# Key norms read from the diagonal of K K^T, queues reordered at the start, and expert weights split without extra copies

## The chip, the cores and the metric

One Trainium2 chip, one core of it. The metric is the device time of one execution in microseconds. In the text PE is the tensor engine (PEld its weight loads), DVE the vector engine, ACT the scalar engine, POOL the GpSimd engine and SP the engine that issues the DMAs.

## What is computed

A delta-rule attention over 4 batches x 8 heads, 768 positions, head size 48, and on its output a dense layer pair 384 -> 2048 -> 384 with softplus between. Cut to what matters:

```python
k_n = k / (norm(k) + 1e-6)
for t in range(768):
    y[t] = q[t] @ state
    v_old = state applied to k_n[t]
    state += beta[t] * outer(k_n[t], v[t] - v_old)
x = y as (3072, 384)
h = x @ w_in
g = maximum(h, 0) + log1p(exp(-abs(h)))
out = g @ w_out
```

`w_in` and `w_out` come as float64 words (`wts`, seen as pairs of int32) and are turned into float32 on the chip.

## The kernel before, in words

**Attention.** The 768 positions are cut into 12 chunks `s` of 64. Inside a chunk the recurrence is a triangular system per head; two chunks make a pair `u`, and the systems of a pair, 32x32 blocks of all heads, are inverted together on DVE. Steps of a chunk: `gram` (products K K^T: the diagonal 32x32 blocks go to `LTD`, the block below them to `OFF`), `norms` (squares on ACT, a row sum on DVE, then a root by Ln and Exp on ACT and one Newton step on DVE; from it the scale `cT` = beta / norm^2 and its negative `ncT`), `invert` (a transpose of `LTD` into `lq`, a mask from POOL times `ncT`, then a substitution loop, L224 and L230), `finish` (two transposes into `tt`), for the first two pairs `join` (the substitution ran over 16x16 blocks there), then `cross_a`, `arrange`, `cross_b`, `keys`, `mask_keys`, `u_all`, `y_all` and `state`. `y_all` leaves the chunk's output as `x` and, for a quarter of the heads, as `x4`, which six small DMAs (L377) lay into `x`.

**The dense layers** (`moe`) take the same 12 chunks of rows, each in 8 groups of two weight slices `f`: products into `ph` (L479), softplus (L483 to L485 on ACT, L493 or L487 on DVE), products into `po` (L462). Chunk 0 multiplies in plain float32 by `HF`; chunks 1 to 11 use three products of split operands (`W` with high and low part).

**Weights.** `weights` converts slice after slice, four DVE passes (L410, L413, L417, L420) between an ACT pass (L398) and an ACT copy into `HF` (L423). `split`, called in chunk 1, copies `HF` on ACT (L430), casts the copy to the high part on ACT (L432) and subtracts on DVE (L433). A one-column DVE copy (L408) holds the load of slice f + AHEAD back until the conversion has come so far.

**What sets the order.** Everything up to the first chunk's output is written out by hand in one block, `with tc.manual_schedule(...)`: there the engines named keep the order of the code, and `fill(n)` puts n steps of the weight conversion in between. Behind it, `attend` and `invert_some` deal attention units and substitution steps out over the groups of the dense layers (`RATE`, `LEAD`, `FIRST`), and a scheduler lays the instructions of an engine in order. Each engine runs its own list in order.

Of the kernel before, what the change touches and what calls it, by code (L numbers as in the profile page):

```python
# [30 lines left out]
AHEAD = 4  # L31
# [4 lines left out]
def deltanet_moe(ctx, tc, kT, qT, kN, kI, vN, beta, wts, out):  # L36
# [35 lines left out]
    bet = const.tile([P, NS, NP], F32, name="bet")  # L72
# [37 lines left out]
    def copy_diagonals(s, pas):  # L110
        u, j = divmod(s, 2)
        for e in range(2):
            nc.scalar.copy(parity(LTD[u][:, j * NP:(j + 1) * NP])[:, e], pas[e][:, :, 0:HB])

    def copy_below(s, pas):
        for e in range(2):
            for h in range(2):
                nc.scalar.copy(parity(OFF[s])[hi[h], e], pas[e][hi[h], :, 0:HB])

    def gram(s):  # L120
        if s not in OFF:
            OFF[s] = two.tile([P, NP, HB], F32, name="off", bufs=3)
# [7 lines left out]
        u, j = divmod(s, 2)  # L130
        for e in range(2):
            nc.scalar.copy(parity(LTD[u][:, j * NP:(j + 1) * NP])[:, e], pas[e][:, :, 0:HB])
        for e in range(2):
            nc.scalar.copy(parity(OFF[s])[:, e], pas[e][:, :, HB:])

    def gram_diagonal(s, pool, name):
        pas = [pool.tile([P, NP // 2, HB], F32, name=name) for e in range(2)]
        for half in (lo, hi):
            for i, e, p, ab, t in quads:
                k = kts[s % 3][dr[ab], p, half[0].start:half[0].stop]  # L140
                nc.tensor.matmul(pas[e][half[t], i, :], k, k, start=True, stop=True)
        copy_diagonals(s, pas)

    def gram_below(s):
        OFF[s] = two.tile([P, NP, HB], F32, name="off", bufs=3)
        pas = [ps_a.tile([P, NP // 2, HB], F32, name="pa") for e in range(2)]
        for i, e, p, ab, t in quads:
            k = kts[s % 3][dr[ab], p, :]
            nc.tensor.matmul(pas[e][hi[t], i, :], k[:, HB:C], k[:, 0:HB], start=True, stop=True)
        copy_below(s, pas)  # L150

    def norms(u, kas=None):

        ss = one.tile([P, 2 * NP], F32, name="ss")
        for j in range(2):
            ka = kas[j] if kas else load_ka(2 * u + j)
            if not kas:
                yield
            nc.scalar.activation(ka, ka, AF.Square)
            yield  # L160
            nc.vector.tensor_reduce(ss[:, j * NP:(j + 1) * NP], ka, op=ALU.add, axis=AX.X)
            yield
        x0 = one.tile([P, 2 * NP], F32, name="rt")
        r0 = one.tile([P, 2 * NP], F32, name="r0")
        nn = two.tile([P, 2 * NP], F32, name="nn")
# [19 lines left out]
        return cT, ncT

    def invert(u, cT, ncT):
# [5 lines left out]
        lq = one.tile([P, HB, HB], F32, name="ltq")  # L193
        for a in blocks:
            nc.gpsimd.affine_select(
                out=Z[:, a:a + n, a:a + n],
                in_=ncT[:, a:a + n].unsqueeze(1).to_broadcast([P, n, n]),
                compare_op=ALU.is_gt, fill=0.0, base=0, pattern=[[1, n], [-1, n]],
                channel_multiplier=0)
        nc.vector.transpose(lq.rearrange("p j i -> p i j"), LTD[u].rearrange("p q i -> p i q"))  # L200
        yield
        for a in blocks:
            d = (slice(None), slice(a, a + n), slice(a, a + n))
            nc.vector.tensor_tensor(lq[d], lq[d], Z[d], op=ALU.mult)
# [86 lines left out]
    def keys(s, e):  # L291

        kt = kts[s % 3]
        for g in range(2):
            pk = ps_a.tile([P, 4, QW], F32, name="pa")
            for i, f, p, ab, t in quads:
                if f == e and i // 4 == g:
                    nc.tensor.matmul(pk[tk[t], i % 4, :], kt[dr[ab], p, :], bv[dr[ab], ab, p, :],  # L298
                                     start=True, stop=True)
            r = parity(NV[s])[:, e, 4 * g:4 * g + 4]  # L300
            nc.vector.tensor_tensor(r, r, pk[:, :, C:], op=ALU.subtract)  # L301
            PK[s, e, g] = pk

    def mask_keys(s, e):

        for g in range(2):
            pk = PK.pop((s, e, g))
            for ab in range(2):
                t = tk[ab ^ e]
                nc.vector.tensor_tensor(  # L310
                    be[tk[ab], ab, e, 4 * g:4 * g + 4, 0:C], pk[t, :, 0:C],
# [37 lines left out]
    def y_all(s):  # L349
# [21 lines left out]
        if s + 1 < NS:  # L371
            load_q(s + 1)
        if n == 2:
            x, x4 = x.bitcast(F32), x4.bitcast(F32)
        for hh in range(NK):
            for ab in range(2):
                nc.sync.dma_start(x[ab * C + D:(ab + 1) * C, :, hh],  # L377
                                  x4[ab * C + 16 * hh:ab * C + 16 * hh + 16])
        return last


    def load_weights(f):
        if f not in ST:
            ST[f] = one.tile([P, 4 * DM], I32, name=f"w{f}")
        nc.sync.dma_start(ST[f], wts[f])

    def weights():
# [8 lines left out]
        def magnitude(f):  # L396
            ex = two.tile([P, 2 * DM], I32, name="ex", bufs=3)
# [3 lines left out]
        ex = magnitude(0)  # L401
        yield
        for f in range(NF):
            hw, lw = words(f)
            if f + AHEAD < NF:

                ST[f + AHEAD] = one.tile([P, 4 * DM], I32, name=f"w{f + AHEAD}")
# [7 lines left out]
            after = magnitude(f + 1) if f + 1 < NF else None  # L415
# [8 lines left out]
            done[0], ex = f + 1, after  # L424
            yield

    def split(f):

        hf = two.tile([P, 2 * DM], F32, name="ex", bufs=3)
        nc.scalar.copy(hf, HF[f])  # L430
        w = W[f] = one.tile([P, 2, 2 * DM], F32R, name=f"w{f}")
        nc.scalar.copy(w[:, 0], hf)  # L432
        nc.vector.tensor_tensor(w[:, 1], hf, w[:, 0], op=ALU.subtract)  # L433


    def moe():
# [4 lines left out]
        for s in range(NS):  # L441
# [10 lines left out]
            def outp(f0, g, po=po, s=s, weight=weight):  # L452
# [64 lines left out]
    cols = {}  # L517
# [11 lines left out]
    def chunk(s):  # L529
        more = s % 2 == 0 and 2 <= s < NS - 2  # L530
        if s % 2 == 0:
            load_v(s + 1)
            if more:
                load_k(s + 2)
                nm = norms(s // 2 + 1)
                next(nm)
            yield from begin(s)
        for e in range(2):
            keys(s, e)
        for e in range(2):  # L540
            mask_keys(s, e)
# [6 lines left out]
        if more:  # L548

            for _ in range(3):  # L550
                next(nm)
        yield
        last = y_all(s)
        if s + 1 < NS:
# [3 lines left out]
        if s + 1 < NS:  # L558
            state(s)
            load_ki(s + 1)  # L560
            if more:
                with tc.issue_after(last[0].ins):
                    next(nm)
                with tc.issue_after(last[1].ins):
                    next(nm)
            yield
        if more:
# [4 lines left out]
            cols[u] = run(nm)  # L572
# [3 lines left out]
            background.append(invert(u, *cols[u]))  # L576

    background, softplus = [], [None]
# [8 lines left out]
    kas = [one.tile([P, 2, NP, D], F32, name=name) for name in ("tt", "x2")]  # L587
    kas = [[t[:, j] for j in range(2)] for t in kas]
    with tc.manual_schedule(engines={ET.PE, ET.DVE, ET.Activation, ET.Pool}):
        for s in range(2):  # L590
            load_k(s)
            nc.sync.dma_start(kas[0][s], kN[s])
# [24 lines left out]
        nm = norms(0, kas[0])  # L617
        for _ in range(5):
            next(nm)
        gram_diagonal(0, ps_a, "pa")  # L620
        gram_diagonal(1, ps_a, "pa")
        cols[0] = run(nm)
        iv = invert(0, *cols[0])
        next(iv)
# [10 lines left out]
        for _ in range(5):  # L635
# [160 lines left out]
```

## Time and profile before

| | us |
|---|---|
| median of 3 runs | 676.06 |
| lowest, highest of 3 runs | 675.17, 678.13 |
| the profiled execution | 672.85 |
| its span in the trace | 671.10 |
| PE busy, share of the span | 611.4, 91% |
| DVE busy | 462.2, 69% |
| ACT busy | 362.1, 54% |

A row of a list of groups names the source line, the engine, the operation, what it writes from what it reads, then the busy time, the mean duration of one instruction, and the idle time of the engine ahead of it with what ended it. "Issue" there is time in which an engine waited for nothing that the profile shows. A float32 product shows in the records twice. The granted clock is a share of the full TensorE clock.

### The profile page before, as it was taken

How to read it: one execution, taken by the hardware profiler on the slowest of the kernel's cores; microseconds unless marked ns; L12 is line 12 of the kernel's file. 1: busy time of each engine (PE TensorE's matmuls, PEld its weight loads, DVE VectorE, ACT ScalarE, POOL GpSimd, SP SyncE). 2: the span in 40 equal slices, each digit the busy share in tenths (PEclk: the TensorE clock that was granted, in tenths of full speed). 3: DMA queues.
4: the chain of work that ended last, by engine and by line, in shares of the span. 5: the costliest groups of instructions: out<-in, count | busy, mean ns of one | idle time of the engine just before them, and what ended most of it. 6: DMA issues, size and time to landing. Idle time of an engine off the chain costs nothing.

```text
span 671.1 us, 22732 instructions
## 1 busy us (share of the span) xinstructions
PE 611.4 (91%) x10032; PEld 570.8 (85%) x10032; DVE 462.2 (69%) x1036; ACT 362.1 (54%) x667; POOL 30.4 (5%) x56
## 2 busy tenths in 40 slices
PE   4356987988989999989999999999999998999997
PEld 3345765678879999979999999998999997999997
DVE  4946499997556986558987559984559884544443
ACT  4234658889563447453555654555545546364433
POOL 3100010000000001000001000001000001000000
PEclk9999887998998999999999999996999998999999
DMA  9826267000131020141211321201202100200000
GB/s 230 272 94 164 101 214 208 0 26 3 51 93 63 26 60 27 49 109 48 58 40 39 92 66 48 60 25 50 61 14 66 30 25 4 61 24 13 3 23 24
DMA packets 35091, 44.73 MB, mean 67 GB/s; under 512 B 21776, under 2 KB 27184, under 8 KB 34992
## 3 DMA queue, kind: packets, MB, share of 16 engines
q1 hardware_dynamic: 34992, 43.27, 22.6%
q8 instruction: 79, 1.29, 0.8%
q14 instruction: 20, 0.16, 0.1%
HBM read 36.27 MB, written 4.72 MB: 61 GB/s over the span
## 4 chain that ended last, share of the span: by engine, by line
PE 77%; DVE 8%; issue 6%; ACT 6%; DMA 2%; SPq 1%; DVEq 0%; ACTq 0%
PE ph L479 28%; PE po L462 28%; PE pa L298 4%; PE pa L359 4%; PE pa L344 2%; PE pa L128 2%; PE pa L285 2%; PE pa L332 2%; PE pa L264 1%; DVE big L310 1%; PE pa L254 1%; ACT tt L276 1%; DMA ka<-kN 1%; DVE tt L237 1%; DMA kt<-kT 1%
## 5 line engine op out<-in xcount | busy, mean ns | idle before, releaser
L479 PE MATMUL ph<-x,w 128*128 128x256 f32 x1680 | 240.5, 294 | 6.1 <-ACT w L423 4.3
L479 PEld LDWEIGHTS ph<-x,w 128*128 128x128 f32 x1680 | 224.0, 192 | 14.7 <-ACT w L423 5.0
L462 PE MATMUL po<-w,gh 128*128 128x384 f32 x768 | 207.0, 355 | 2.1 <-DVE gh L493 1.6
L483 ACT ACTIVATE a<-ph 128x512 f32<-128x512 f32 x96 | 57.4, 598 | 167.7 <-PE ph L479 164.4
L462 PEld LDWEIGHTS po<-w,gh 128*128 128x128 f32 x768 | 134.9, 190 | 12.0 <-DVE gh L493 2.4
L487 DVE SCALAR_TENSOR_TENSOR a<-ph,a 128x512 f32<-128x512 f32 x88 | 60.5, 689 | 107.0 <-ACT a L485 105.9
L462 PE MATMUL po<-w,gl 128*128 128x384 f32 x352 | 119.5, 340 | 0.0
L462 PEld LDWEIGHTS po<-w,gl 128*128 128x128 f32 x352 | 66.5, 189 | 0.6 <-DVE gl L490 0.2
L490 DVE TENSOR_TENSOR gl<-a,gh 128x512 fp32r<-128x512 f32 x88 | 60.8, 691 | 3.3 <-DVE Z L230 0.2
L484 ACT ACTIVATE a<-a 128x512 f32<-128x512 f32 x96 | 60.8, 633 | 2.7
L485 ACT ACTIVATE a<-a 128x512 f32<-128x512 f32 x96 | 60.7, 632 | 2.3
L230 DVE TENSOR_TENSOR Z<-Z,work 128x84 f32<-128x84 f32 (+14 forms) x148 | 44.2, 306 | 2.9
L224 DVE TENSOR_TENSOR work<-Z,ltq 128x84 f32<-128x84 f32 (+14 forms) x148 | 44.1, 305 | 2.4
L489 DVE CAST gh<-a 128x512 fp32r<-128x512 f32 x88 | 37.5, 427 | 7.8 <-PE po L462 5.6
L298 PE MATMUL pa<-big,kt 48*64 48x112 f32 x704 | 39.3, 284 | 0.0
L310 DVE TENSOR_TENSOR big<-pa,maskP 64x256 f32<-64x256 f32 x88 | 37.0, 420 | 1.4
L298 PEld LDWEIGHTS pa<-big,kt 48*64 48x64 f32 x704 | 35.2, 148 | 1.7 <-issue 0.8
L336 ACT COPY big<-pa 64x384 f32<-64x384 f32 x46 | 21.6, 472 | 26.7 <-PE pa L332 26.0
L359 PEld LDWEIGHTS pa<-big 128*64 128x64 f32 x768 | 28.9, 154 | 5.4 <-ACT big L336 2.0
L359 PE MATMUL pa<-big 128*64 128x64 f32 x768 | 32.0, 243 | 1.5 <-ACT big L336 1.2
L278 POOL MEMSET tt<- 32x512 f32 x24 | 13.1, 544 | 400.3 <-PE pa L264 219.3
L301 DVE TENSOR_TENSOR nv<-nv,pa 128x192 f32<-128x192 f32 x44 | 15.3, 352 | 19.1 <-PE pa L298 18.3
(101 smaller groups left out, 611.9 us busy)
## 6 DMA issues: line engine op xcount, KB each, us to landing
w<-wts SPq DMA_DIRECT2D x16, 768.0 KB, 5.9
kt<-kT SPq DMA_DIRECT2D x24, 192.0 KB, 3.6
big<-qT SPq DMA_DIRECT2D x24, 192.0 KB, 3.8
nv<-vN SPq DMA_DIRECT2D x12, 384.0 KB, 3.4
ki<-kI SPq DMA_DIRECT2D x24, 192.0 KB, 3.5
out<-ex SPq DMA_DIRECT2D x24, 192.0 KB, 1.9
ka<-kN SPq DMA_DIRECT2D x8, 384.0 KB, 3.9
x<-x SPq DMA_DIRECT2D x66, 32.0 KB, 2.4
```

What stands on the lines that cost most here:

```text
L224: nc.vector.tensor_tensor(tmp[:, a:a + r, 0:j], Z[:, a + j + 1:a + n, a + j:a + j + 1].to_broadcast([P, r, j]), lq[:, a + j:a + j + 1, a:a ...
L230: nc.vector.tensor_tensor(z, z, tmp[:, a:a + r, 0:j], op=ALU.add)
L298: nc.tensor.matmul(pk[tk[t], i % 4, :], kt[dr[ab], p, :], bv[dr[ab], ab, p, :], start=True, stop=True)
L310: nc.vector.tensor_tensor(be[tk[ab], ab, e, 4 * g:4 * g + 4, 0:C], pk[t, :, 0:C], maskP[t].unsqueeze(1).to_broadcast([C, 4, C]), op=ALU.mult)
L359: nc.tensor.matmul(py[tk[ab], i, :], big[:, at + C:at + 2 * C], big[:, at:at + C], start=True, stop=True)
L462: nc.tensor.matmul(po[:, h, 0:DM], g[b][:, f - f0, h * P:(h + 1) * P], weight(f, a, DM, DM), start=(f == 0 and i == 0), stop=end)
L479: nc.tensor.matmul(ph[:, f - f0], weight(f, a, k * P, P), xr[b][k], start=(c == 0), stop=(c == len(terms1) * NK - 1))
L483: nc.scalar.activation(a, ph, AF.Abs)
L484: nc.scalar.activation(a, a, AF.Exp, scale=-1.0)
L485: nc.scalar.activation(a, a, AF.Ln, bias=1.0)
L487: nc.vector.scalar_tensor_tensor(a, ph, 0.0, a, op0=ALU.max, op1=ALU.add)
L490: softplus[0] = nc.vector.tensor_tensor(g[1], a, g[0], op=ALU.subtract)
```

## The change

- **Norms.** The array `kN`, its loads, the squares and the row sums are gone. `gram_heads` multiplies each head's whole 48x64 key block with itself: 32 products of 64x64 in a chunk, where `gram` had 64 products with 32 weight columns. `invert` transposes `LTD` first, then a strided copy takes the diagonal as the squared norms, POOL clears the diagonal and what lies above it in place, and `norms` goes on in the transposed layout. All of it is now part of the inversion's own steps.
- **Copies of the gram.** A 64x64 product holds its two diagonal blocks in different columns, so `copy_diagonals` makes three copies where one was; for the first two chunks ACT and DVE take half of them each.
- **Start.** SP is now in the hand-written block. The keys of chunks 0 and 1 are loaded first, then weight slice 0; `load_q(1)` stands behind the six small `x` DMAs of chunk 0; the first group of the dense layers stands ahead of `join(1)`; conversion steps are dealt out anew.
- **Weights.** The last conversion pass writes in place into `ST[f]`, which then is `HF[f]`; `split` casts and subtracts straight from it. Slice f lives in buffer `w{f+1}`, so `W[0]` has a free buffer at once, and each later `W[f]` takes the buffer of the slice ahead of it. AHEAD is 3, it was 4.

The core of the diff:

```diff
-    def gram(s):
-        for i, e, p, ab, t in quads:
-            k = kts[s % 3][dr[ab], p, :]
-            for half, order in ((lo, k), (hi, k.rearrange("d (b c) -> d b c", b=2)[:, ::-1, :])):
-                first = half[0].start
-                nc.tensor.matmul(pas[e][half[t], i, :], k[:, first:first + HB], order,
-                                 start=True, stop=True)
+    def gram_heads(s):
+        pas = [ps_a.tile([P, NP // 2, C], F32, name="pa") for e in range(2)]
+        for i, e, p, ab, t in quads:
+            k = kts[s % 3][dr[ab], p, :]
+            nc.tensor.matmul(pas[e][tk[t], i, :], k, k, start=True, stop=True)
+        return pas
...
+            copies[e](ltd[:, e], pas[e][:, :, HB:])
+            for h in range(2):
+                copies[e](ltd[lo[h], e], pas[e][lo[h], :, 0:HB])
...
-            nc.scalar.activation(ka, ka, AF.Square)
-            nc.vector.tensor_reduce(ss[:, j * NP:(j + 1) * NP], ka, op=ALU.add, axis=AX.X)
+        nc.vector.tensor_copy(ss, lq.rearrange("p j i -> p (j i)")[:, 0:HB * HB:HB + 1])
...
-    def invert(u, cT, ncT):
-            nc.gpsimd.affine_select(out=Z[:, a:a + n, a:a + n], in_=ncT[:, a:a + n]...
+    def invert(u):
+        nc.vector.transpose(lq.rearrange("p j i -> p i j"), LTD[u].rearrange("p q i -> p i q"))
+        yield
+        nm = norms(u, lq)
+        next(nm)
+            nc.gpsimd.affine_select(out=lq[d], in_=lq[d], compare_op=ALU.is_gt, fill=0.0, ...
+        cT, ncT = yield from nm
...
-        if s + 1 < NS:
+        if 0 < s < NS - 1:
             load_q(s + 1)
         ...
+        if s == 0:
+            load_q(1)
...
-            nc.vector.scalar_tensor_tensor(ex, lw, 29, ex, op0=ALU.logical_shift_right,
+            nc.vector.scalar_tensor_tensor(ST[f][:, 0:2 * DM], lw, 29, ex, op0=ALU.logical_shift_right,
                                            op1=ALU.bitwise_or)
-            HF[f] = one.tile([P, 2 * DM], F32, name=f"w{f}")
-            nc.scalar.copy(HF[f], ex.bitcast(F32))
+            HF[f] = ST[f][:, 0:2 * DM].bitcast(F32)
...
-        hf = two.tile([P, 2 * DM], F32, name="ex", bufs=3)
-        nc.scalar.copy(hf, HF[f])
         w = W[f] = one.tile([P, 2, 2 * DM], F32R, name=f"w{f}")
-        nc.scalar.copy(w[:, 0], hf)
-        nc.vector.tensor_tensor(w[:, 1], hf, w[:, 0], op=ALU.subtract)
+        nc.scalar.copy(w[:, 0], HF[f])
+        nc.vector.tensor_tensor(w[:, 1], HF[f], w[:, 0], op=ALU.subtract)
...
         y_all(0)
+        load_k(3)
+        load_v(1)
+        fill(5)
+        state(0)
+        load_ki(1)
+        next(mg)
         jn = join(1)
```

How the lists of the engines move, at the three places that the prediction speaks of.

**DVE, the start of its list.** Before, up to the transpose of the first pair's blocks (`ss` holds the squared norms, `nn` the norms, `ltq` the transposed blocks):

```order
L161 TENSOR_REDUCE ss<-tt 128x16 x2
L166 TENSOR_SCALAR rt<-ss 128x32
L170 RECIPROCAL r_132<-rt 128x32
L171 TENSOR_TENSOR r_132<-r_132,ss 128x32
L172 TENSOR_TENSOR r_132<-r_132,rt 128x32
L173 TENSOR_SCALAR nn<-r_132 128x32
L177 TENSOR_TENSOR r_132<-nn 128x32
L178 RECIPROCAL r_132<-r_132 128x32
L179 TENSOR_TENSOR r_132<-r_132,bet 128x32
L183 STREAM_TRANSPOSE cT<-r_132 128x32
L184 TENSOR_SCALAR ncT<-cT 128x32
L200 STREAM_TRANSPOSE ltq<-work 128x32x32
```

The same place in the changed kernel:

```order
L116 COPY work<-pa 128x8x32
L118 COPY work<-pa 32x8x32 x2
L116 COPY work<-pa 128x8x32
L118 COPY work<-pa 32x8x32 x2
L166 STREAM_TRANSPOSE ltq<-work 128x32x32
L133 COPY ss<-ltq 128x32
L138 TENSOR_SCALAR rt<-ss 128x32
L388 COPY w_217<-ex 128x1
L390 TENSOR_SCALAR ex<-ex 128x768
L393 TENSOR_SCALAR ex<-ex 128x768
L142 RECIPROCAL r_206<-rt 128x32
L143 TENSOR_TENSOR r_206<-r_206,ss 128x32
```

The transpose stood behind the norms and now stands ahead of them; copies of the gram come first, and one slice's first two conversion passes stand where DVE waits for ACT's Ln and Exp.

**PE, from chunk 0's output to the first products of the dense layers.** Before (L359 is `y_all`, L247 and L254 are `join`, L344 is `state`, L479 the dense layers):

```order
L359 MATMUL pa<-big 64x64 x32
L247 MATMUL pa<-tt,x_303 32x16 x64
L344 MATMUL pa<-big,ki 48x48 x32
L254 MATMUL pa<-x_303,tt 32x16 x64
L479 MATMUL ph<-x_847,w_706 128x256 x3
```

The same place in the changed kernel (L336 is `y_all`, L321 `state`, L457 the dense layers, L225 and L232 `join`):

```order
L336 MATMUL pa<-big 64x64 x32
L321 MATMUL pa<-big,ki 48x48 x32
L457 MATMUL ph<-x_664,w_89 128x256
L457 MATMUL ph<-x_664,w_104 128x256
L457 MATMUL ph<-x_664,w_89 128x256
L457 MATMUL ph<-x_664,w_104 128x256
L457 MATMUL ph<-x_664,w_89 128x256
L457 MATMUL ph<-x_664,w_100 128x256 x3
L225 MATMUL pa<-tt,x_284 32x16 x64
```

`join(1)`, 128 products, stood between chunk 0's output and the first dense products and now stands behind the first group of them.

**DVE, inside the conversion.** In the changed kernel, some ten conversion passes after the first softplus (L390, L393, L398 and L401 are the four passes, L411 the subtraction of `split`, whose line before was L433):

```order
L393 TENSOR_SCALAR ex<-ex 128x768
L398 SCALAR_TENSOR_TENSOR ex<-w_617,ex 128x768
L411 TENSOR_TENSOR w_1498<-w_100,w_1498 128x768
L401 SCALAR_TENSOR_TENSOR w_617<-w_617,ex 128x768
L388 COPY w_969<-ex 128x1
L411 TENSOR_TENSOR w_1501<-w_104,w_1501 128x768
L390 TENSOR_SCALAR ex<-ex 128x768
L94 TENSOR_TENSOR nv<-nv,nn 128x768
```

Before, one L433 stood ahead of the last conversion pass of all 16 slices, and 15 behind it; now 13 subtractions stand ahead of it and 3 behind it.

## Rows read from the trace of the kernel before

**Rows 1.** Windows: stretch, then each engine's busy us, granted clock, DMA share, GB/s.

```profile
0.00:67.00 67.00, 32.42 (x1409) 29.03 (x1409) 43.06 (x114) 24.73 (x48) 10.71 (x26) 0.98 0.67 190
67.00:129.00 62.00, 54.16 (x653) 41.35 (x647) 52.86 (x101) 43.94 (x74) 3.93 (x6) 0.89 0.46 142
...
134.00:206.00 72.00, 64.37 (x1583) 59.96 (x1581) 49.49 (x121) 49.43 (x89) 3.51 (x5) 0.94 0.16 44
206.00:671.00 465.00, 455.67 (x6380) 437.16 (x6380) 311.84 (x683) 239.07 (x449) 12.25 (x19) 0.98 0.16 43
```

**Rows 2.** Timeline, PE, up to the first dense products: start, us, line, count, idle before.

```profile
4.93 1.84 PE L141 MATMUL pa<-kt 48*32 48x32 f32 x126 [0.84 <-DMA kt<-kT]
...
20.85 2.08 PE L318 MATMUL ph<-big,kt 48*64 48x64 f32 x34 [4.16 <-issue]
...
28.93 0.61 PE L247 MATMUL pa<-tt,x 32*32 32x16 f32 x28
...
33.70 1.57 PE L247 MATMUL pa<-tt,x 32*32 32x16 f32 x100 [4.16 <-issue]
...
35.73 0.61 PE L254 MATMUL pa<-x,tt 32*32 32x16 f32 x28 [0.46 <-ACT x L249]
39.22 1.57 PE L254 MATMUL pa<-x,tt 32*32 32x16 f32 x100 [2.88 <-issue]
...
66.34 0.73 PE L254 MATMUL pa<-x,tt 32*32 32x16 f32 x39 [3.19 <-issue]
67.00 6.39 PE L479 MATMUL ph<-x,w 128*128 128x256 f32 x20
```

**Rows 3.** Timeline, DVE, the first pair's norms and inversion.

```profile
11.88 0.35 DVE L170 RECIPROCAL r<-rt 128x32 f32<-128x32 f32 x1 [0.56 <-ACT rt L168]
...
14.34 2.12 DVE L200 STREAM_TRANSPOSE ltq<-work 128x1024 f32<-128x1024 f32 x1
...
19.57 0.24 DVE L224 TENSOR_TENSOR x<-Z,ltq 128x14 f32<-128x14 f32 x2
...
26.32 1.95 DVE L236 STREAM_TRANSPOSE tt<-Z 128x1024 f32<-128x1024 f32 x1
```

**Rows 4.** Groups of instructions: busy us, mean ns of one, idle before and releaser.

```profile
L417 DVE SCALAR_TENSOR_TENSOR ex<-w,ex 128x768 int32<-128x768 int32 x16 | 15.3, 958 | 0.2
L413 DVE TENSOR_SCALAR ex<-ex 128x768 int32<-128x768 int32 x16 | 9.1, 573 | 0.1
L433 DVE TENSOR_TENSOR w<-ex,w 128x768 fp32r<-128x768 f32 x16 | 15.1, 955 | 3.2 <-ACT w L432 3.2
L161 DVE TENSOR_REDUCE ss<-ka 128x16 f32<-128x768 f32 x8 | 7.6, 949 | 7.5 <-ACT ka L159 7.5
L118 ACT COPY off<-pa 32x256 f32<-32x256 f32 x8 | 2.9, 363 | 7.5 <-PE pa L149 7.3
```

**Rows 5.** Timeline, ACT, SP and DVE around chunk 0's output, and the last conversion pass.

```profile
44.80 0.83 ACT L423 COPY w<-ex 128x768 f32<-128x768 f32 x1 [8.33 <-DVE ex L420]
...
58.45 1.67 SPq L83 DMA_DIRECT2D big<-qT  x2
...
60.22 3.80 SPq L377 DMA_DIRECT2D x<-x  x6
...
73.65 0.69 DVE L493 SCALAR_TENSOR_TENSOR gh<-ph,a 128x512 f32<-128x512 f32 x1 [3.92 <-ACT a L485]
...
128.22 0.98 DVE L420 SCALAR_TENSOR_TENSOR ex<-w,ex 128x768 int32<-128x768 int32 x1
```

**Rows 6.** PE behind the conversion: a group of lines, then the timeline's products of `keys`.

```profile
L128 PE MATMUL pa<-kt 48*32 48x64 f32 x1024 | 12.7, 225 | 5.3 <-issue 5.3
...
175.37 2.96 PE L298 MATMUL pa<-big,kt 48*64 48x112 f32 x64
...
200.38 5.56 PE L298 MATMUL pa<-big,kt 48*64 48x112 f32 x64
```

**Rows 7.** Timeline, PE's weight loads of `cross_a` for pair 2.

```profile
255.88 1.15 PEld L264 LDWEIGHTS pa<-tt,off 32*32 32x32 f32 x66 [0.27 <-DVE tt L236]
```

More of the change, by code (lines that the diff above doesn't have):

```diff
@@ L30, with deltanet_moe @@
 QB = HB // 2
-AHEAD = 4
+AHEAD = 3
 N16 = 2
 @with_exitstack
-def deltanet_moe(ctx, tc, kT, qT, kN, kI, vN, beta, wts, out):
+def deltanet_moe(ctx, tc, kT, qT, kI, vN, beta, wts, out):
     nc = tc.nc
@@ new lines, in gram_heads, with copy_diagonals, copy_below @@
+        return pas
+    def copy_diagonals(s, pas, copies=(nc.scalar.copy, nc.scalar.copy)):
+        ltd = parity(LTD[s // 2][:, s % 2 * NP:(s % 2 + 1) * NP])
+        for e in range(2):
+            copies[e](ltd[:, e], pas[e][:, :, HB:])
+            for h in range(2):
+                copies[e](ltd[lo[h], e], pas[e][lo[h], :, 0:HB])
+    def copy_below(s, pas):
+        OFF[s] = two.tile([P, NP, HB], F32, name="off", bufs=3)
+        for e in range(2):
+            nc.scalar.copy(parity(OFF[s])[:, e], pas[e][:, :, 0:HB])
@@ L166, in norms, with gram @@
+    def gram(s):
+        pas = gram_heads(s)
+        copy_diagonals(s, pas)
+        copy_below(s, pas)
+    def norms(u, lq):
+        ss = one.tile([P, HB], F32, name="ss")
+        nc.vector.tensor_copy(ss, lq.rearrange("p j i -> p (j i)")[:, 0:HB * HB:HB + 1])
+        x0 = one.tile([P, HB], F32, name="rt")
+        r0 = one.tile([P, HB], F32, name="r0")
+        nt = one.tile([P, HB], F32, name="nt")
+        nn = two.tile([P, HB], F32, name="nn")
         nc.vector.tensor_scalar(x0, ss, 1e-30, None, op0=ALU.max)
@@ L288, in cross_b, with keys, mask_keys @@
             copies[s < 1 and h](tt[lo[h], :, HB:], pm[lo[h]])
-    def keys(s, e):
+    def keys(s, g):
         kt = kts[s % 3]
[L294 to L299, printed above, removed]
-            r = parity(NV[s])[:, e, 4 * g:4 * g + 4]
[L301 to L307, printed above, removed]
+        pks = PK[s, g] = [ps_a.tile([P, 4, QW], F32, name="pa") for e in range(2)]
+        for i, e, p, ab, t in quads:
+            if i // 4 == g:
+                nc.tensor.matmul(pks[e][tk[t], i % 4, :], kt[dr[ab], p, :], bv[dr[ab], ab, p, :],
+                                 start=True, stop=True)
+        for e in range(2):
+            r = parity(NV[s])[:, e, 4 * g:4 * g + 4]
+            nc.vector.tensor_tensor(r, r, pks[e][:, :, C:], op=ALU.subtract)
+    def mask_keys(s, g):
+        pks = PK.pop((s, g))
+        for e in range(2):
             for ab in range(2):
@@ L534, in chunk @@
                 load_k(s + 2)
-                nm = norms(s // 2 + 1)
-                next(nm)
             yield from begin(s)
[L538 to L541, printed above, removed]
+        for g in range(2):
+            keys(s, g)
+        for g in range(2):
+            mask_keys(s, g)
         yield
@@ L547, in chunk @@
             cross_b(s + 1)
-        if more:
-            for _ in range(3):
-                next(nm)
         yield
         last = y_all(s)
-        if s + 1 < NS:
+        if s % 2 == 0:
             with tc.issue_after(last[1].ins):
@@ L560, in chunk @@
             load_ki(s + 1)
[L561 to L565, printed above, removed]
             yield
@@ L585, in invert_some @@
                     background.pop()
[L587 to L592, printed above, removed]
+    with tc.manual_schedule(engines={ET.PE, ET.DVE, ET.Activation, ET.Pool, ET.SP}):
+        load_k(0)
+        load_k(1)
+        load_weights(0)
         nc.sync.dma_start(bet, beta)
@@ L616, in deltanet_moe @@
         systems(0)
-        nm = norms(0, kas[0])
-        for _ in range(5):
[L619 to L624, printed above, removed]
+        pas = [gram_heads(s) for s in range(2)]
+        for s in range(2):
+            copy_diagonals(s, pas[s], copies)
+        iv = invert(0)
+        next(iv)
+        next(conversion)
+        copy_below(0, pas[0])
+        next(iv)
+        copy_below(1, pas[1])
+        fill(2)
+        for _ in range(5):
+            next(iv)
         nc.gpsimd.memset(maskP, 1.0)
@@ L634, in deltanet_moe @@
                                     pattern=[[0, NP], [1, D]], channel_multiplier=-1)
-        for _ in range(5):
-            next(iv)
-        gram_below(0)
         pts = [p_half(0, g, ps_h, "ph") for g in range(2)]
-        gram_below(1)
-        load_k(3)
-        next(conversion)
         run(iv)
@@ L645, in deltanet_moe @@
         finish(0)
-        nm = norms(1, kas[1])
-        next(nm)
         jn = join(0)
@@ L657, in deltanet_moe @@
         arrange(0)
+        fill(3)
+        cross_b(0)
         fill(2)
-        cross_b(0)
+        u_all(0)
         fill(3)
-        u_all(0)
-        next(nm)
-        fill(4)
         y_all(0)
+        load_k(3)
[4 more added lines that the diff above has]
+        next(mg)
         jn = join(1)
@@ L673, in deltanet_moe @@
         fill(2)
-        for _ in range(3):
-            next(nm)
-        fill(3)
         scale_v(1)
@@ L679, in deltanet_moe @@
         load_v(2)
-        cols[1] = run(nm)
         fill(3)
@@ L684, in attention @@
         nonlocal steps_done
-        for e in range(2):
-            keys(1, e)
-        for e in range(2):
-            mask_keys(1, e)
+        for g in range(2):
+            keys(1, g)
+        for g in range(2):
+            mask_keys(1, g)
         yield
@@ L692, in attention @@
         last = y_all(1)
-        with tc.issue_after(last[1].ins):
-            scale_v(2)
         yield
```

112 lines of the change are left out of this document (35 added, 77 removed).

## The prediction

> **What bounds the kernel now.** I read the windows first, then the waits and the timeline of each stretch. PE is the fullest engine, but not evenly. Behind 206 us it is busy 455.67 of 465 us: there PE is the bound, and only fewer or faster products count. Ahead of 67 us it is busy 32.42 of 67 us; from 67 to 129 us DVE is the fuller engine, 52.86 of 62 us; from 134 to 206 us PE loses 7.6 us and runs at a granted clock of 0.94 [rows 1]. So the change can earn its time ahead of 206 us. The weights are the reason that DVE bounds the second stretch: four passes a slice, two near 0.96 us and two near 0.57 us, 3.05 us for each of 16 slices [rows 4], the last ending at 129.2 us [rows 5], and PE cannot do the last group of chunk 0 before that.
>
> The stretch up to 67 us is a chain: keys, norms, substitution, `join(0)`, chunk 0's output, its DMAs, the first dense products. In it PE waits for "issue" again and again, 4.16, 4.16, 2.88 and 3.19 us in the rows shown [rows 2]. Between the waits of `join(0)` lie 100 products of L247 and 28 of L254, 128 recorded products. A stop at a fixed count, with no engine named, I read as PE's own instruction list arriving late. The Trainium skill, "Runtime: NRT & Kernel Launch", section "Instruction fetch mechanics", says that the list is refilled in blocks of 256 instructions, which is 128 products with their weight loads, and agrees on the count. It also says that this is mostly hidden, by which the 5 us of part 2 and the 1 us of part 5 would not come; the waits of 2.88 to 4.16 us speak against that, and the sum goes by the rows.
>
> **The change, part by part.** Times below are positions in the profiled execution, which took 672.85 us, 3.2 us under the median of 676.06.
>
> *1. Front, until the first pair's substitution ends (before: 26.3 us [rows 3]).* The gram must now be complete before norms can start. A chunk's 32 products are 64 records. No row has this form in this place; the nearest are L318, 61 ns a record at 20.85 us [rows 2], and L298, whose 112 columns take 46 or 87 ns a record [rows 6], 26 or 50 ns for 64 columns. I take 50, since products this early run slowly, so 3.2 us a chunk (1.7 to 3.9). With the first keys there at 4.93 us [rows 2], both chunks end at 11.3 us. Copies add 1.1 us (three of some 0.36 us [rows 4], half on DVE), the transpose 2.1, the diagonal's copy and a maximum 0.7; while ACT does Ln and Exp, DVE does 1.3 us of conversion; the nine small steps take 2.4 us (11.88 to 14.34 before), scaling 3.0 (16.5 to 19.57), substitution 6.75 (19.57 to 26.32) [rows 3]. That ends at 28.6 us: **2.3 us later** (0.5 earlier to 4 later), of which 1.3 us is conversion that DVE owed anyway. POOL's select runs beside these steps and, if it did not, would add its own half microsecond or so twice.
>
> *2. From there to the first dense products (67.0 us before).* `gram` and `gram_diagonal` cost PE 512 records for three chunks and the lower blocks; now it is 192. By the count of 128, `join(0)` then meets one stop where it met two, 4.16 and 2.88 us [rows 2]: 5 us less (4 to 7). The ACT copy L423, which waited for DVE until 44.80 us [rows 5] with `cross_a`'s copy queued behind it, goes: 1.7 us less. One split, 0.83 us of ACT and 0.96 of DVE, now stands ahead of `cross_b`'s copies: 0.5 us more. Then `join(1)` and its stop of 3.19 us no longer stand ahead of L479, and the six `x` DMAs no longer wait for the 1.67 us of q's [rows 5]: 3 us less (2 to 5); what is late next is those DMAs themselves, 3.80 us of issue [rows 5] and a landing. On SP, q, k, v and two weight slices stand behind them now; a slice's load starts three slices ahead of its use, some 12 us at 3.05 us and a split each, so I book nothing for them or for AHEAD; if it falls short, ACT waits for a slice and the stretch of part 3 grows by that. Together 9 us less, with part 1 **7 us less**: dense products begin near 60 us.
>
> *3. Until the last conversion pass (129.2 us).* That gain is no gain of the whole, since DVE bounds this stretch. DVE was busy 43.06 + 52.86 = 95.9 us of 129 and idle 33 [rows 1]. Gone are five row sums (4.7 us [rows 4]), a scaling and some of pair 1's steps that now come later (3.4), one split (1.0). New are 13 splits at 0.955 us [rows 4], 12.4 us, gram copies 2.3 and small ones 1.2: 102.7 us. Idle time I put at 25 us: 9 until the gram's copies, 6 in the chain to chunk 0's output, 8.5 for the first softplus (which came at 73.65 us [rows 5]), 1.5 for the second. So the last pass ends at 128 us: **1 us less**. But 13 slices are then split, not one.
>
> *4. Chunk 1 of the dense layers (134 to 206 us).* The ACT copies L423 and L430 and the late splits leave this stretch; ACT was busy 49.43 of 72 us here, DVE 49.49, PE 64.37 [rows 1]. PE's idle 7.6 us includes one issue stop of 3.0 us behind L128 (part 5), and some 4 us lie in slow products: `keys` took 5.56 us where it took 2.96 us at 175 us [rows 6]. I take 5.5 of the 7.6 us and 1 us of the slow ones: **6.5 us less** (3 to 10).
>
> *5. Behind 206 us.* Eight more grams. L128 takes 12.7 us of busy time for eight, 1.6 us each, and 5.3 us in two stops [rows 6], of which one, 2.3 us, lies behind 206 us. The new form at 26 ns a record is 1.7 us: nothing, as PE pays it in full. The Trainium skill, "TensorEngine Tiling (Array Packing)", section "Available Configurations", gives eight tiles of 64x32 and four of 64x64, so the new products would get half the concurrency; as each does two old ones' work, its estimate is 1.6 us as well. Half the records in the same time should spare the stop: **1 us less** (3 less to 3 more, were the stops to move elsewhere).
>
> Sum: 1 + 6.5 + 1 = 8.5 us less. Against the profiled 672.85 that is 664.4, against the median 667.6; I say **666 us**. The squares and row sums behind 206 us cost nothing today, being beside PE's work, as do the loads of kN; no gain is booked for them.
>
> **Rivals.**
> *The splits get in the way.* An error of 7 us in the 102.7, some 0.06 us for each of about 120 steps that overlap their neighbours less than today's, would end the last pass at 135 us and start chunk 1 6 us late; part 4 wins that back and no more. For it: 13 splits do stand ahead. Against: ACT is lighter. End: 672 to 677 us, no change. Chance 0.16.
>
> *More than I booked.* DVE's idle time falls to 20 us, and the slow products of chunk 1 run at the full clock: 5 us and 3 us more, 652 to 659 us. Chance 0.13.
>
> *Slower: the inversion comes late.* From pair 2 on, `norms` lay far ahead; now they stand between the transpose and the scaling: Ln and Exp on ACT behind a softplus triple, nine small DVE steps and POOL's select, some 6 us together. PE's `cross_a` was already released by the inversion's end, a wait of 0.27 us [rows 7]. The list puts `cross_a` about 0.75 groups later, 4.4 us at 465 us for the 80 groups of ten chunks [rows 1]. If the inversion is more than that late, PE waits at each of four pairs; at 4 us each and no recovery, and with chunk 2's start hit too, 16 to 20 us: 680 to 687 us. Against it: DVE and ACT have a third of their time free there. Chance 0.10.
>
> **How the numbers follow.** My forecast, 660 to 672 us, has 0.61. One measurement can tell about 0.5% from no change, 3.4 us, so faster means below 672.7: 0.61 + 0.13 = 0.74; same 0.16; slower 0.10. The range 655 to 677 us leaves out the slower rival and half of the better one, with the tails.
>
> **What would show it.** Right: L457 begins near 60 us; the stops of `join(0)` fall to one; the last L401 ends at 126 to 131 us with 13 L411 ahead of it; chunk 1's dense products take 62 to 67 us instead of 72; the stretch behind is as long as before within 3 us. Wrong: the last L401 beyond 133 us (first rival), L242 waiting for L214 or L215 by over 2 us at each pair (third), or the gram's 64 records over 3 us behind 206 us.

## The result, and the profile after

| | before | after |
|---|---|---|
| median, us | 675.69 (4 runs, 675.17 to 678.13) | 659.20 (4 runs, 657.56 to 660.08) |
| ratio | | 0.9746, 95% interval 0.9714 to 0.9779 |
| the profiled execution, its span | 672.85, 671.10 | 657.56, 655.8 |
| PE, DVE, ACT busy | 611.4, 462.2, 362.1 | 596.3, 456.5, 346.6 |

16.5 us less, where 10 were forecast. Executions of one kernel differ by up to 2% here; medians in this text are of all runs, and the ratios leave out runs more than 1.5% above the fastest of their kernel. The timeline of PE after; the lines answer to [rows 2, 6] (L110 is the gram, L225 and L232 `join`, L457 and L440 the dense layers):

```profile
5.06 3.97 PE L110 MATMUL pa<-kt 48*64 48x64 f32 x126 [0.52 <-DMA kt<-kT]
...
29.27 1.90 PE L225 MATMUL pa<-tt,x 32*32 32x16 f32 x128 [11.33 <-DVE tt L214]
31.66 1.47 PE L232 MATMUL pa<-x,tt 32*32 32x16 f32 x92 [0.48 <-ACT x L227]
33.96 0.72 PE L232 MATMUL pa<-x,tt 32*32 32x16 f32 x36 [0.83 <-issue]
...
53.86 2.34 PE L457 MATMUL ph<-x,w 128*128 128x256 f32 x8 [1.35 <-DMA x<-x]
...
61.82 1.24 PE L232 MATMUL pa<-x,tt 32*32 32x16 f32 x127
67.71 0.18 PE L232 MATMUL pa<-x,tt 32*32 32x16 f32 x1 [4.65 <-issue]
67.82 5.04 PE L440 MATMUL po<-w,gh 128*128 128x384 f32 x8
...
123.16 2.59 PE L457 MATMUL ph<-x,w 128*128 128x256 f32 x6 [3.53 <-issue]
...
190.25 2.54 PE L110 MATMUL pa<-kt 48*64 48x64 f32 x128
...
471.30 1.16 PE L110 MATMUL pa<-kt 48*64 48x64 f32 x64
```

The first dense product starts at 53.86 us, before at 67.00. `join(0)` stops once, for 0.83 us. A new stop of 4.65 us stands at the last record of `join(1)`. The wait of 3.53 us at 123.16 has no releaser named, but the timeline of DVE has one (L401 is the last pass over a slice):

```profile
122.11 0.94 DVE L401 SCALAR_TENSOR_TENSOR w<-w,ex 128x768 int32<-128x768 int32 x1
...
126.00 0.96 DVE L401 SCALAR_TENSOR_TENSOR w<-w,ex 128x768 int32<-128x768 int32 x1
```

A pass ends at 123.05 us, 0.1 us ahead of the products that need its slice: the end of chunk 0 still hangs on DVE. Windows by stage after, columns as in [rows 1]:

```profile
0.00:54.00 54.00, 27.35 (x833) 25.09 (x834) 43.16 (x117) 20.44 (x43) 11.49 (x28) 0.72 0.50 136
54.00:127.00 73.00, 57.34 (x845) 41.08 (x846) 60.28 (x105) 43.52 (x74) 6.90 (x4) 0.93 0.55 162
127.00:200.00 73.00, 65.91 (x1486) 59.59 (x1485) 44.87 (x130) 37.43 (x75) 2.24 (x4) 0.98 0.14 35
200.00:656.00 456.00, 445.66 (x5977) 427.26 (x5975) 308.15 (x689) 245.17 (x470) 13.52 (x20) 0.98 0.15 40
```

The start of a chunk's output DMAs marks its end. Chunk 0 ends 0.5 us sooner than before (138.1 for 138.6), chunk 1 9.1 us sooner, chunk 9 15.3 us sooner. So 8.6 us were won in chunk 1 and 6.2 us behind it. Chunk 1 before and after, windows:

```profile
138.60:211.20 72.60, 64.97 (x1591) 61.35 (x1590) 47.09 (x96) 49.36 (x89) 3.51 (x5) 0.93 0.18 49
```

```profile
138.10:202.10 64.00, 60.37 (x1465) 55.99 (x1465) 36.19 (x96) 34.14 (x69) 2.24 (x4) 0.98 0.17 43
```

Behind chunk 1 the groups of PE products stand at (L275 is `keys`, L242 `cross_a`):

```profile
L275 PE MATMUL pa<-big,kt 48*64 48x112 f32 x512 | 22.4, 274 | 1.3 <-ACT off L123 1.2
...
L242 PE MATMUL pa<-tt,off 32*32 32x32 f32 x512 | 8.9, 191 | 0.0
L110 PE MATMUL pa<-kt 48*64 48x64 f32 x384 | 7.1, 221 | 0.0
```

`keys` comes in a new order with this change, which the list of changes above does not name: all four places of the array in turn, where before only two alternated. In the kernel before it was 27.2 us behind 206 us, so it was the first suspect for the 6.2 us, the gram the second.

### The profile page after: what moved, and what is told of

Read it like the earlier page. It is cut to its first block, busy times and chain, and to the rows that moved or that the text cites. A ratio compares the mean times of both kernels' runs of the same rounds, so it can differ in the third digit from the quotient of the medians.

```text
span 655.8 us, 20943 instructions
## 1 busy us (share of the span) xinstructions
PE 596.3 (91%) x9136; PEld 553.0 (84%) x9136; DVE 456.5 (70%) x1037; ACT 346.6 (53%) x661; POOL 34.2 (5%) x56
## 4 chain that ended last, share of the span: by engine, by line
PE 75%; DVE 12%; ACT 7%; issue 3%; DMA 3%; SPq 1%; ACTq 0%; DVEq 0%
PE ph L457 30%; PE po L440 29%; PE pa L336 4%; PE pa L275 2%; PE pa L321 2%; PE pa L309 2%; ACT tt L254 2%; PE pa L263 2%; DVE big L287 1%; PE pa L110 1%; DVE tt L215 1%; DMA w<-wts 1%; DVE tt L214 1%; PE pa L232 1%; PE pa L225 1%
## 5 line engine op out<-in xcount | busy, mean ns | idle before, releaser
L457 PE MATMUL ph<-x,w 128*128 128x256 f32 x1680 | 240.6, 292 | 8.6 <-issue 5.2
L457 PEld LDWEIGHTS ph<-x,w 128*128 128x128 f32 x1680 | 222.3, 191 | 16.9 <-issue 7.4
L440 PE MATMUL po<-w,gh 128*128 128x384 f32 x768 | 209.4, 358 | 7.0 <-DVE gh L471 5.6
L440 PEld LDWEIGHTS po<-w,gh 128*128 128x128 f32 x768 | 135.9, 191 | 22.6 <-issue 7.3
L440 PE MATMUL po<-w,gl 128*128 128x384 f32 x352 | 119.0, 338 | 0.0
L440 PEld LDWEIGHTS po<-w,gl 128*128 128x128 f32 x352 | 66.1, 188 | 0.9 <-DVE gl L468 0.6
L275 PE MATMUL pa<-big,kt 48*64 48x112 f32 x704 | 30.9, 271 | 3.4 <-ACT off L123 2.6
L336 PEld LDWEIGHTS pa<-big 128*64 128x64 f32 x768 | 27.6, 152 | 4.6 <-ACT big L313 1.2
L336 PE MATMUL pa<-big 128*64 128x64 f32 x768 | 30.2, 240 | 0.9 <-ACT big L313 0.7
L275 PEld LDWEIGHTS pa<-big,kt 48*64 48x64 f32 x704 | 25.1, 138 | 6.8 <-ACT off L123 4.5
```

Of the source, the lines that this page charges most:

```text
L275: nc.tensor.matmul(pks[e][tk[t], i % 4, :], kt[dr[ab], p, :], bv[dr[ab], ab, p, :], start=True, stop=True)
L336: nc.tensor.matmul(py[tk[ab], i, :], big[:, at + C:at + 2 * C], big[:, at:at + C], start=True, stop=True)
L440: nc.tensor.matmul(po[:, h, 0:DM], g[b][:, f - f0, h * P:(h + 1) * P], weight(f, a, DM, DM), start=(f == 0 and i == 0), stop=end)
L457: nc.tensor.matmul(ph[:, f - f0], weight(f, a, k * P, P), xr[b][k], start=(c == 0), stop=(c == len(terms1) * NK - 1))
```

## Experiments

Ratios are against runs of the kernel before on the same chip. The lengths come from one profiled execution each; of four kernels it lay 4 us or more above their median, and their lengths are left out. Times in us:

| run | median | ratio, 95% interval | first dense product | last conversion pass (splits ahead) | end of chunk 0 | chunk 1, its clock | chunks 2 to 9 |
|---|---|---|---|---|---|---|---|
| before | 675.69 | | 67.00 | 129.2 (1) | 138.6 | 72.6, 0.93 | 390.9 |
| after | 659.20 | 0.9746 (0.9714 to 0.9779) | 53.86 | 127.0 (13) | 138.1 | 64.0, 0.98 | 384.7 |
| e11, after again | 659.77 | 0.9781 (0.9725 to 0.9837) | 52.90 | 126.6 (13) | 139.0 | 66.0, 0.93 | 387.5 |
| e1, old `keys` | 656.90 | 0.9783 (0.9726 to 0.9839) | 53.00 | 122.5 (11) | 131.1 | 65.2, 0.97 | 387.9 |
| e2, before + new `keys` | 674.83 | 1.0004 (0.9966 to 1.0041) | | | | | |
| e3, old gram | 669.64 | 0.9937 (0.9904 to 0.9969) | 55.25 | | | | |
| e4, both old | 669.48 | 0.9953 (0.9911 to 0.9995) | 54.74 | | | | |
| e10, old gram everywhere | 668.52 | 0.9900 (0.9852 to 0.9947) | 59.50 | 126.9 (10) | 137.9 | 66.5, 0.95 | 391.1 |
| e5, splits late | 660.02 | 0.9844 (0.9769 to 0.9920) | 55.91 | 121.1 (0) | 131.0 | 73.7, 0.86 | 388.5 |
| e6, old start order | 657.72 | 0.9819 (0.9752 to 0.9885) | 56.73 | 117.2 (11) | 128.9 | 66.9, 0.93 | 393.5 |
| e12, `join(1)` first | 659.57 | 0.9724 (0.9656 to 0.9792) | 56.25 | 119.4 (11) | 132.3 | 69.6, 0.89 | 386.9 |
| e7, 40 records more | 662.49 | 0.9878 (0.9788 to 0.9968) | 56.01 | 128.5 (13) | 139.5 | 64.7, 0.95 | 388.6 |
| e8, before, in place | 678.18 | 1.0122 (1.0056 to 1.0188) | 64.25 | 127.1 (2) | 141.5 | 74.7, 0.89 | 390.0 |
| e9, splits on POOL | 669.32 | 0.9839 (0.9759 to 0.9919) | 57.87 | | | | |

### The order of `keys`: e1 and e2

```diff
-        for g in range(2):
-            keys(s, g)
+        for e in range(2):
+            keys(s, e)
```

> The changed kernel with keys and mask_keys in their order of before (one parity e of the heads at a time, so that products alternate between two places of the array, where the changed order goes through four). Theory (the order of the products sets how many run side by side, and PE is the bound behind chunk 0): keys behind 206 us goes back from 22.4 to about 27 us, and with the chunks ahead of it the time rises by 5 to 8 us, to 664 to 667. Rival (keys got cheaper by the clock or by what stands around it, not by its order): keys stays near 22 us and the time within 1.5 us of 659.

> The kernel before with the changed order of keys and mask_keys alone. Theory (order of the products): 5 to 8 us less, 668 to 671, keys behind 206 us from 27 to 22.5 us. Rival (not the order): 675 within 1.5 us.

e1's group shows the records dearer by 6.3 us, as the theory had it:

```profile
L276 PE MATMUL pa<-big,kt 48*64 48x112 f32 x512 | 28.7, 277 | 0.9 <-ACT off L123 0.8
```

The time did not follow: e1's ratio cannot be told from after's (0.9783 for 0.9746, e11 0.9781), and e2's interval leaves at most 2.3 us to the new order. **My theory fell.** The 6.3 us of busy time bought nothing that these runs can tell; e1's chunks 2 to 9 take 387.9 us, those of after 384.7 and 387.5.

### The form of the gram: e3, e4 and e10

```diff
-            nc.tensor.matmul(pas[e][tk[t], i, :], k, k, start=True, stop=True)
+            for half, order in ((lo, k), (hi, k.rearrange("d (b c) -> d b c", b=2)[:, ::-1, :])):
+                nc.tensor.matmul(pas[e][half[t], i, :], k[:, first:first + HB], order, ...
```

> The changed kernel with the gram of chunks 2 to 11 in its form of before: 64 products with 32 weight columns and four ACT copies in place of 32 products of 64x64 and eight copies. Chunks 0 and 1 keep the new form. Theory (half the records at less than twice the time each, and one stop for the instruction list less): gram behind 206 us from 7.1 to about 9.6 us and a stop of 2 to 3 us more, the time 3 to 5 us up, 662 to 664. Rival (my prediction's term: the two forms cost PE the same, and a stop only moves): 658 to 660.5.

> The changed kernel with both undone, keys in the old order and the old gram for chunks 2 to 11. Theory (two separate costs of PE): the rises of the two single runs add up, 8 to 13 us, 667 to 672, and what is left against the kernel before is the first 200 us. Rival (the two share one cause, such as where the stops of the instruction list fall): no more than the larger of the two alone.

> The changed kernel with the old gram for all 12 chunks, the first two among them: 128 products and four copies at the start where the change has 64 products and six copies, behind which the norms from the diagonal stay. Theory (the gain of the first 200 us comes from PE's list being shorter, with fewer stops for it): one or two stops of 2 to 4 us more ahead of the first dense product, which starts at 57 to 61 us where the run with the old gram from chunk 2 on had 55.25; 668 to 674 us. Rival (the front's gain comes from the chain of norms and the order, not from the gram's records): first dense product within 1 us of 55.25 and the time within 2 us of 669.6.

The old gram costs far more than I had expected of it: e3 is 2.0% above after by the two ratios, some 13 us, which neither side had; e4 is the same within the intervals (again nothing for `keys`); and e10, run on the same chip as e11, lies 8.7 us above it. The copies are not the reason, since the old form needs four on ACT where the new one needs eight. The start is not the reason: e10's first dense product comes 6.6 us later than in e11, at 59.50, and its chunk 0 ends 1.1 us sooner. e10's own rows on PE (L142 is the old gram):

```profile
116.20 0.33 PE L142 MATMUL pa<-kt 48*32 48x64 f32 x10 [3.55 <-issue]
...
191.94 2.61 PE L142 MATMUL pa<-kt 48*32 48x64 f32 x196
196.38 0.82 PE L142 MATMUL pa<-kt 48*32 48x64 f32 x60 [1.84 <-issue]
...
293.02 0.66 PE L142 MATMUL pa<-kt 48*32 48x64 f32 x41 [1.47 <-issue]
...
480.35 1.48 PE L142 MATMUL pa<-kt 48*32 48x64 f32 x128
```

Two chunks' grams take 5.3 us from 191.94 with their stop; after, the same two take 2.54. Without a stop a chunk is 1.48 us against 1.16. Three stops (6.9 us) and ten times 0.3 us make 9.9 us, the most that these rows can explain; the first stop lies beside DVE's conversion, and since chunk 0 ends no later, it seems to cost nothing. Behind it the rows give some 6 us. The intervals of e10 and e11 together leave about 5 us either way on the 8.7, so the prices are of the right order. More is not shown: the two profiled executions, 666.26 and 663.27 us, lie only 3.0 us apart, and no run separates the stops from the price of a record.

### Where the splits stand: e5 and e9

```diff
+        with tc.issue_after(lastconv[0].ins):
+            nc.vector.tensor_tensor(w[:, 1], HF[f], w[:, 0], op=ALU.subtract)
```

> The changed kernel with every subtraction of split held back on DVE until the last conversion pass. Theory (chunk 0 is bound by DVE, and 13 subtractions of 0.955 us ahead of the last pass lengthen it): the last pass ends 8 to 12 us sooner than 126.96 us, at 115 to 119, chunk 1's first dense products start by 122, and the time falls by 2 to 7 us, 652 to 657. Rival (the subtractions stood in DVE's idle time, or what is won in chunk 0 is paid in chunk 1, which then waits for them): chunk 0 ends at most 4 us sooner, or does and chunk 1 takes as much longer; 658 to 666.

The windows of e5 up to the end of chunk 0, and of its chunk 1:

```profile
56.00:131.00 75.00, 65.02 (x891) 47.65 (x892) 58.59 (x120) 41.28 (x73) 4.89 (x4) 0.93 0.51 157
131.00:204.70 73.70, 66.58 (x1458) 61.36 (x1458) 45.43 (x116) 41.89 (x80) 2.07 (x4) 0.86 0.16 40
```

Thirteen subtractions fewer end the conversion 5.8 us sooner, chunk 0 7.1 us sooner, and chunk 1 takes 9.7 us more. The rival holds as to the sum: the time stays. It does not show that the subtractions alone fill chunk 1: of its 9.7 us, PE's idle time is 3.5 (7.1 for 3.6) and PE's busy time 6.2, at a granted clock of 0.86 for 0.98. e9 has the start of e12 (e6, with which its expectation compares, also has `load_q(1)` moved) and gives 12 of the subtractions to POOL:

```diff
+        (nc.gpsimd if f > 3 else nc.vector).tensor_tensor(w[:, 1], HF[f], w[:, 0], op=ALU.subtract)
```

> The changed kernel with join(1) ahead of the first dense group again and, new, the subtraction of 12 of the 16 splits on POOL, which is 5% busy. Theory (DVE bounds chunk 0, and each subtraction ahead of the last conversion pass costs it 0.955 us): the last conversion pass ends at 105 to 112 us where the run with join(1) first alone had 117.16, chunk 1's output comes 4 to 8 us sooner than that run's 195.8 us, the time 648 to 654. Rival (PE and the chain of softplus hold chunk 0, or POOL's subtraction is so long that chunk 1 waits for it): last pass at 114 or later, or chunk 1 longer by what chunk 0 gains; 655 to 662.

The group of e9's subtractions on POOL, and rows of DVE's timeline:

```profile
L411 POOL TENSOR_TENSOR w<-w,w 128x768 fp32r<-128x768 f32 x12 | 24.3, 2021 | 45.7 <-ACT w L410 43.0 <-DVE a L465 1.8 <-DVE Z L208 0.9
```

```profile
92.67 2.17 DVE L390 TENSOR_SCALAR ex<-ex 128x768 f32<-128x768 f32 x1
...
102.98 2.56 DVE L398 SCALAR_TENSOR_TENSOR ex<-w,ex 128x768 int32<-128x768 int32 x1
...
119.84 1.78 DVE L143 TENSOR_TENSOR r<-r,ss 128x32 f32<-128x32 f32 x1
```

POOL's subtraction takes 2021 ns, where DVE's took 955 [rows 4]. POOL's subtractions that start at 92.42, 102.53 and 118.97 us lie beside these three DVE instructions. Each lasts some 1.6 us longer than its like elsewhere in the same profile (0.55, 0.94) or in after's (L143, 0.17). Of the four passes of all slices, two of L390 and three of L398 are held up so; the rest keep their length. So much of the relief is lost again: the last pass came at 119.9 us, no sooner than in e12 (119.4). e9's ratio of 0.9839 shows no gain over e12's 0.9724 or after's 0.9746.

### The start order: e6, e12 and e7

```diff
-        next(mg)
         jn = join(1)
         next(jn)
         fill(4)
         run(jn)
+        next(mg)
```

e12 is this alone; e6 also puts `load_q(1)` back ahead of the x DMAs.

> The changed kernel with part of its start order undone: join(1) ahead of the first dense group, and load_q(1) ahead of the six small x DMAs, as before. Theory (part 3 of the prediction: DVE's conversion sets the end of chunk 0, so an earlier first dense product is worth little): the first dense products start 4 to 8 us later than 53.86 us, the last conversion pass ends within 2 us of 126.96, the time rises by 0 to 2 us. Rival (the start passes through to the end): 4 to 8 us up, 663 to 667.

> The changed kernel with one line moved: join(1) ahead of the first dense group as before; load_q(1) stays behind the six small x DMAs. It is also the version that the earlier runs point to. Theory (with the first group ahead of it, the second half of join(1) meets the stop of 4.65 us at its last record, DVE and PE's next group wait behind it, and those products then run at the lower clock): no stop over 2 us behind 50 us and before 80 us, chunk 0's output at 128 to 133 us and chunk 1's at 194 to 199, where the changed kernel's two profiles have 138 to 139 and 202 to 205; the time 653 to 657.5. Rival (what is won there is given back in chunk 1 and by the clock behind it): chunk 1's output by 201 or later, or the time 658 to 662.

e12 on PE at the place of the 4.65 us stop, and its windows:

```profile
55.04 1.28 PE L232 MATMUL pa<-x,tt 32*32 32x16 f32 x103 [1.59 <-issue]
56.25 6.08 PE L457 MATMUL ph<-x,w 128*128 128x256 f32 x20
```

```profile
54.00:132.30 78.30, 65.32 (x729) 47.97 (x730) 69.68 (x149) 47.96 (x82) 6.10 (x4) 0.88 0.52 150
132.30:201.90 69.60, 64.46 (x1465) 60.33 (x1465) 34.51 (x85) 34.15 (x70) 2.25 (x4) 0.89 0.16 40
```

The long stop is gone, the dense products start 2.4 us later (e6: 2.9), and the last pass ends 7.6 us sooner (e6: 9.8), of which two subtractions fewer ahead of it are 1.9; the rest is not settled. That a later start comes with a sooner last pass, neither side of e6's expectation had. Yet chunk 1 gives nearly all of it back in e12, at a granted clock of 0.89 for after's 0.98. Neither time can be told from after's, so e12 beats the kernel before, but not the change. That the clock fell because PE reached chunk 1 sooner was not tried.

e7 runs the last 20 products of chunk 1's gram twice, 40 records more:

```diff
+        for i, e, p, ab, t in quads[-20:]:
+            k = kts[1][dr[ab], p, :]
+            nc.tensor.matmul(pas[1][e][tk[t], i, :], k, k, start=True, stop=True)
```

> The changed kernel with the last 20 products of chunk 1's gram run a second time at the start, 40 records more on PE's list ahead of everything else. Theory (stops come at a fixed count of PE's instruction list): the stop inside the second half of join(0) comes 40 records sooner, after about 52 of its records instead of 92, and the stop of 4.65 us, now at the last record of the second half of join(1), falls some 40 records sooner, inside it. Rival (the stops belong to those instructions or to what they wait for): both stay at the same record. The time within 2 us of 659 in either case.

```profile
32.64 0.93 PE L232 MATMUL pa<-x,tt 32*32 32x16 f32 x52 [0.48 <-ACT x L227]
34.44 1.25 PE L232 MATMUL pa<-x,tt 32*32 32x16 f32 x76 [0.87 <-issue]
...
63.27 0.91 PE L232 MATMUL pa<-x,tt 32*32 32x16 f32 x87
68.18 0.73 PE L232 MATMUL pa<-x,tt 32*32 32x16 f32 x41 [4.00 <-issue]
```

Both stops came exactly 40 records sooner, behind 52 records for 92 and behind 87 for 127. They belong to a count in PE's list and to nothing that these products wait for. The time, 662.49 us, lies above the 659 within 2 that both sides had; the ratio of 0.9878 is clear of after's 0.9746 but not of e11's 0.9781 for the same kernel, so a price of the shift is not shown. The Trainium skill, "Runtime: NRT & Kernel Launch", section "Instruction fetch mechanics", says that such refills are mostly hidden; among short products these were not.

### The conversion in place alone, and after once more: e8 and e11

```diff
-            HF[f] = one.tile([P, 2 * DM], F32, name=f"w{f}")
-            nc.scalar.copy(HF[f], ex.bitcast(F32))
+            HF[f] = ST[f][:, 0:2 * DM].bitcast(F32)
```

> The kernel before with the last conversion pass writing in place, so that ACT's copy of each slice (16 of 0.83 us) is gone; split, buffers and order stay as before. Theory (ACT's copies held chunk 0's and chunk 1's chains a little): 1 to 4 us less, 671.5 to 674.5. Rival (they were hidden beside DVE's passes): 675.5 within 1 us.

e8 is slower by 1.2%, which neither side had. Its first dense product comes 2.75 us sooner and its last pass 2.1 us, but chunks 0 and 1 end 2.9 and 5.0 us later. From the first dense product to the end of chunk 0, PE stands idle 11.9 us for 8.1 (6.2 of it in one wait for `gh`) at a granted clock of 0.85 for 0.90. Why isn't settled. It does say that taking ACT's 16 copies into `HF` out of the kernel before gains nothing by itself.

> The changed kernel once more, without an edit, for its times beside the other runs of this call and for a second profile. If the lengths of its chunks in the first profile are its own, the second has the chunks behind 202 us at 40.6 to 59.4 us each, within 0.5 us, and chunk 0's output at 138 us; if the granted clock makes them, chunks with a clock under 1.00 differ by 2 to 5 us and those at 1.00 by under 0.5 us. The time 656 to 662.

Chunk 3 in the profile of after and in that of e11, windows:

```profile
244.50:298.00 53.50, 51.89 (x935) 48.54 (x934) 30.08 (x63) 32.06 (x65) 2.08 (x4) 1.00 0.19 51
```

```profile
247.50:305.50 58.00, 56.38 (x935) 52.55 (x934) 30.06 (x63) 31.99 (x65) 2.07 (x4) 0.91 0.18 47
```

The same products, 4.5 us apart at a clock of 0.91 for 1.00. Chunk 9 goes the other way, 59.4 us at 0.91 and 57.5 at 0.97; the other chunks from 2 to 8 agree within 0.2 us. So of the 6.2 us behind chunk 1 in the first profile, 2.8 go with the clock of that execution: the second has 3.4.

## Why the prediction held, point by point

The time lay in the range of 655 to 677 us and the sign was right, at 659 for 666 us, just under the 660 to 672 that had a chance of 0.61. The sum of 8.5 us was too small, and two of its terms were mis-sized, parts 4 and 5; that the time stayed so near is partly luck, as part 4 shows. Of the signs named, the first dense product near 60 us and an unchanged stretch behind chunk 1 did not come; the other three did.

- **Part 1.** The substitution ends at 27.2 us; 28.6 was forecast. The gram of two chunks took 3.97 us, 31 ns a record and not the 50 that I took from products further on.
- **Part 2.** The first dense product was put near 60 us and came at 53.86: 13.1 us less for 7. `join(0)`'s stops fell from 7.04 to 0.83 us (6.2 for 5), from `y_all` to the first dense product it took 8.0 us for 13.5 (5.5 for 3), and the front cost 0.9 us, not 2.3. What I missed is what stood next: the stop is not spared but moves on by count: 4.65 us in `join(1)`, where 3.19 stood [rows 2].
- **Part 3.** The last pass at 127.0 us for 128, with 13 subtractions ahead, as forecast. My reason, that DVE swallows the start's gain, was half of it: with the splits held back (e5) 8 of 11 us of the earlier start reach the last pass. The subtractions then take 5.8 us of that, for 12.4 us of DVE's time, so DVE alone did not bound this stretch. The row behind that was misread: from 67 to 129 us PE is the fuller engine, busy 54.16 of 62 us, DVE 52.86 [rows 1].
- **Part 4.** Chunk 1 was to lose 6.5 us; it lost 8.6, in the second profile 6.6. The shares were others. Of PE's idle time 4.0 us went (7.6 to 3.6), where 5.5 were booked; of its busy time 4.6 us went, where 1 was booked, with 126 records fewer and a granted clock of 0.98 for 0.93. In the second profile, at 0.93, the busy time fell by 2.2. So the mechanism is right for the idle time, and the number came near with the clock's help. With the splits back in it (e5) chunk 1 is as long as before (73.7 for 72.6), but at a clock of 0.86.
- **Part 5**, the step that failed: "the new form at 26 ns a record is 1.7 us: nothing". At the full clock a chunk's 64 records take 1.16 us, 18 ns each, and no gram meets a stop, where L128 lost 2.3 us behind 206 us and 3.0 us in chunk 1 [rows 6]. I had scaled the price from `keys`, whose records are nearly twice as wide. Undoing the gram costs 8.7 us (e10 for e11). By the estimate from the Trainium skill, "TensorEngine Tiling (Array Packing)", section "Available Configurations", the two forms would have cost about the same; the rows say otherwise.
- **The rivals.** "More than I booked", 652 to 659, is where it nearly came out, by part 5 rather than by DVE's idle time. "The splits get in the way" holds as a mechanism and not as a price: e5. The slower one did not come: L242 waits 0.0 us behind 200 us; what is new there is 2.1 us of L263 behind ACT's L244.

Of the 16.5 us, then, some 9 hang on the gram's form (8.7 by e10, within about 5; some 13 by e3). The rest lies ahead of 205 us with the new start and the weights: e10, which lacks only the gram, still ends chunk 1 at 204.4 us for 211.2, takes as long as before for chunks 2 to 9 (391.0 for 390.9), and is 1.0% faster than before. How that divides between norms, order and weights no run separates; the in-place pass, the order of `join(1)` and the place of the splits gave no gain that could be measured alone.

## What to carry to other kernels

Count products as well as their time: where many short ones follow each other, PE stops for its list at a fixed count, so half the records can be worth more than their busy time says; here undoing it (e10) cost 8.7 us, where 1 us had been booked for it. Before an order is credited with a busy time that fell, undo it and look at the time. And look at both stages before work is moved from one to the other: without thirteen subtractions chunk 0 took 7.1 us less, with them chunk 1 took 9.7 us more, some of it by a lower clock, and the time stayed.

## What the runs showed of the hardware

- PE's stops move with the count of recorded products, to the record (e7). Behind the one of 4.65 us, eight products of L440 took 5.04 us, at 115.58 us 2.74. In the second profile, where the same eight took 5.49 us behind the same stop, that place had a granted clock of 0.50, the lower level of 1.2 GHz:

```profile
66.00:72.00 6.00, 5.26 (x9) 2.86 (x9) 3.86 (x6) 0.83 (x1) 0.00 (x0) 0.50 0.57 151
```

- Single DVE instructions beside a POOL subtraction of 128x768 take some 1.6 us longer: 2.56 us for 0.94 in a conversion pass, 1.78 for 0.17 in a small step of the norms (e9).
- A chunk's length depends on the granted clock too: chunk 3 took 53.5 us at 1.00 and 58.0 us at 0.91 with the same instructions.
